# Linear-attention layers: two value tiles moved behind the last segment's keys, the first queries' features begun sooner, feature transposes in the two-bank logits tile

## The chip, the cores and the metric

The kernel runs on one core of a Trainium2 chip, as one launch with nothing computed on the host. A core has engines that run at the same time, each with its own instruction stream: PE (TensorE, matrix products and transposes), DVE (VectorE), ACT (ScalarE), POOL (GpSimd) and SP (SyncE, which here issues the transfers). They wait for each other on semaphores. PE writes its products to PSUM, from which DVE and ACT read them; everything else lives in SBUF, and what does not fit goes out to DRAM and comes back. The metric is the device time of one execution in microseconds (us), the median over runs.

## What is computed

A tensor x of 2048 rows (tokens) by 512 columns passes four layers: a linear-attention layer A, a segmented memory-attention layer B, then A and B again with the same weights, each on the layer-normed x and added back to it. There are 32 heads of 16 columns. The change lies in layer A alone:

```python
qkv = x @ wqkv                                   # 512 -> 3 * 512, split into q, k, v of 32 heads x 16
pq  = einsum("bhsd,hdf->bhsf", q, w_phi)         # a 16x16 matrix per head
pk  = einsum("bhsd,hdf->bhsf", k, w_phi)
phi_q = concat([softmax(pq), softmax(-pq)])      # 32 features per head
phi_k = concat([softmax(pk), softmax(-pk)])
kv  = einsum("bhsf,bhsd->bhfd", phi_k, v)        # summed over all 2048 tokens
z   = einsum("bhsf->bhf", phi_k)
num = einsum("bhqf,bhfd->bhqd", phi_q, kv)
den = einsum("bhqf,bhf->bhq", phi_q, z)[..., None] + 1e-6
out = (num / den) @ wo                           # heads side by side again
```

Nothing of `num` can be computed before `kv` holds all tokens, so layer A has two passes.

## The kernel before

**Layer A, first pass** (`LayerA.pass1`). The rows are worked in four segments of four tiles of 128 rows; the segments go in the order 1, 2, 3, 0. For a tile t of a segment, `kproj` and `qproj` multiply the transposed normalised rows by the key or query weights (with the per-head matrix folded in) into a PSUM tile "g", and ACT copies it to SBUF: keys to "U", queries to "tb". `v_tile` makes the value rows of a whole segment, four tiles with 12 matmuls each, in 16 steps (four a tile: three times four matmuls, then ACT's copy). The values of the coming segment are interleaved with the keys and queries of the present one by a list, `plan`: its entries say behind which step of the projections a step of the values, of the norms or of the transposes is taken. Of a query or key tile the features are made in four stages: `extremes` (DVE: maximum and minimum of each head, to `mmq` or `mm`), `differences` (two POOL instructions, to a fresh tile of the pool "P"), `exp` (ACT, in place, 128x1024), and the scaling by the reciprocal sums, `scale_q` for queries (DVE sums `es` and reciprocals `rr`, then one POOL multiplication) and `scale_k` for keys. `kv(0)` and `kv(1)` multiply key features with values into the PSUM tiles mx and my, and DVE adds them to `kva`.

The queries of the first three segments are stored in DRAM unfeatured (`pq`) and come back in the second pass. Those of the last segment, which holds the rows 0 to 511 and so the first four tiles of the second pass, stay in SBUF (`later`), and `begun(t)` takes their extremes and differences: for tiles 0 to 2 in full, for tile 3 the extremes alone.

**Layer A, second pass** (`LayerA.pass2`). At its front `kva` is transposed by PE ("g<-ident,kva") and masked by DVE into `KN`. Then, for each of 16 tiles: `transposed` turns the 128x1024 query features by eight 128x128 PE transposes, in two halves of four, each half copied by ACT to SBUF ("P<-g"); the product with `KN` (32 small matmuls, "g<-KN,P") in two halves; `weigh` divides by the denominator (DVE: reciprocal `r`, product `tmp`); `turn` transposes `tmp` (four PE transposes, "g<-ident,tmp"), which ACT rounds to `oh` and DVE completes by the rest `ol`; `out_proj` multiplies by the output weights (12 matmuls, "g<-w,oh" and "g<-w,ol"), and DVE adds x and SP stores the row tile. The loop runs one tile ahead: in an iteration i PE does turn(i-1), KN(i), transposes(i+1), out_proj(i-1), except for i = 1 and 2, where the transposes stand behind out_proj.

In the second pass's latter half the opening work of the following layer B (norms, projections, first logits) is mixed in at listed steps, and 103 of the second pass's steps run before layer B proper begins; the few that are left are taken in B's first slots.

**What sets the order.** Each engine runs its instructions in the order in which the program writes them: the wrapper `Ordered` (all its instructions carry line L163) and `held` (PE's: L185 for `mm`, L189 for `tp`) tie each instruction behind the one before it on its engine. Waits between engines follow from reads and writes of the same tiles.

**PSUM.** "g" is a set of three tiles of one bank (2 KB a partition) that rotate; "lg" is one tile of two banks, which layer B uses for its logits; mx, my and pv have a bank each:

```python
pt = PS("g", G)                    # one bank, one of three
lg = PS("lg", 1, (P, 2, 512))      # two banks, a single tile
```

**SBUF.** The pool "P" has six buffers of 128x1024, for features and for their transposes; "tb" (raw queries) and "U" (raw keys) two each.

Of the kernel before, what the change touches and what calls it, by code (L numbers as in the profile page):

```python
# [18 lines left out]
P = 128  # L19
NSEG = 4  # L20
# [87 lines left out]
def interleave_kernel(ctx, tc, x_in, a_wqkv, a_wphi, a_wo, b_wq, b_wk, b_wv, b_wo, b_beta,  # L108
# [78 lines left out]
    def tp(*a):  # L187
        work[0] += 108
        return held(nc.tensor.transpose(*a))  # L189
# [371 lines left out]
    def exp(e):  # L561
        ef = e.rearrange("p h s f -> p (h s f)")
        act.activation(ef, ef, AF.Exp)
# [24 lines left out]
    class LayerA:  # L588
# [68 lines left out]
        def pass1(self, first):  # L657
# [35 lines left out]
            for n, s in enumerate(SEGS):  # L693
# [51 lines left out]
                if n < NSEG - 1:  # L745
# [2 lines left out]
                    plan = [(j, g) for j in ((0, 2, 3, 4, 4, 8, 9, 11, 13) if n == 0 and not first else (4, 7, 10, 13))]  # L748
                    vals, norms = [10 + j * 26 // 16 for j in range(16)], (14, 19, 20, 21, 22, 23, 24, 27, 29, 31, 33)
                    vt = v_tile(hTs, wv, vv, ("g", G))  # L750
                    plan += [(j, vt) for j in vals]
                    if n + 2 < NSEG:
                        upc = upcoming(n + 2)
                        plan += [(j, upc[1]) for j in norms]
# [30 lines left out]
                        yield  # L785
                    for _, step in plan:
                        next(step, None)
                    late = kv(1)
                    continue

# [9 lines left out]

                for t in range(8):
                    yield from (kproj(t, e) if t < 4 else qproj(t - 4, e, later))
                    if t == 2:
                        yield from late
                        self.wo = load_w("awo")
                    if 0 < t < 5:
                        exp(e[t - 1])
                    if t in (5, 6):
                        add = kv(t - 5)
                        next(add)  # L810
                    if 1 < t < 6:
                        es.append(scale_k(e[t - 2]))
                    if t == 5:
                        yield from add
                        begun(0)
                    if t == 6:
                        begun(1)
                        exp(e[4])
                        yield from add
                        scale_q(e[4])  # L820

                pt = PS("g", G)
                for i in range(4):
# [2 lines left out]
                for j in (0, 2):  # L826
# [1 line left out]
                                      in0=pt.rearrange("p (g x) -> p g x", x=PW)[:, :, 0 : 2 * VW].rearrange(  # L828
                                          "p g (h e) -> p g h e", e=VW),
                                      in1=bdA[:, j : j + 2].unsqueeze(1).unsqueeze(3).broadcast_to([P, 8, 2, VW]))  # L830
                exp(e[5])
                scale_q(e[5])
                begun(2)
                begun(3)
                self.e = {4 * s + t: e[4 + t] for t in range(3)}
                yield

# [6 lines left out]
        def pass2(self):  # L844

            KN = self.KN
            phT = {}

            def transposed(i):

                if i >= NT:
                    return
                ef = self.e.pop(i).rearrange("p h s f -> p (h s f)")
                phT[i] = T2("P4", NP4, shape=(P, 8, P))
                for half in range(2):
                    pt = PS("g", G)
                    for q in range(4):
                        g = 4 * half + q  # L860
                        tp(pt[:, q * P : (q + 1) * P], ef[:, g * P : (g + 1) * P], ident)
                    act.copy(phT[i][:, 4 * half : 4 * half + 4, :], pt.rearrange("p (g t) -> p g t", g=4))
                    yield

            yield from transposed(0)
            o = None
            for i in range(NT + 1):
                if i > 0:
                    oT = turn([o[:, c * P : (c + 1) * P] for c in range(NC)])
                    yield PAUSE if i == NT else None  # L870
                if i + 2 < NT:
                    exp(self.e[i + 2])
                if i < NT:
                    o = T2("tmp", 2)
                    f = phT.pop(i)
                    for half in range(2):
                        pn = PS("g", G)
                        pv = pn[:, 0 : 16 * VW].rearrange("p (g h e) -> p g h e", g=4, h=4)
                        for q in range(4):
                            g = 4 * half + q  # L880
                            for a in (0, 64):
                                mm(pn[a : a + 64, q * 4 * VW : (q + 1) * 4 * VW], lhsT=f[:, g, a : a + 64],
                                   rhs=KN[:, g].rearrange("p h e -> p (h e)"), start=True, stop=True,
                                   tile_position=(0, a))
                        weigh(o[:, half * 256 : half * 256 + 256].rearrange("p (g h d) -> p g h d", g=4, h=4),
                              pv, 0.0, False)
                        yield
                    if not 0 < i < 3:
                        yield from transposed(i + 1)
                    if i + 2 < NT:  # L890
                        scale_q(self.e[i + 2])
                    if i + 3 < NT:
                        self.e[i + 3] = differences(*self.raw.pop(i + 3))
                    self.load_q(i + 4)
                    ahead = residual(self.xsrc, i, ("ot", OT))
                if i > 0:
                    yield from out_proj(x, self.xdst, i - 1, oT, self.wo)
                if 0 < i < 3:
                    yield from transposed(i + 1)
                x = ahead  # L900


# [468 lines left out]
```

## Time and profile before

| what | us |
|---|---|
| median of three runs | 1523.32 (1521.91 to 1523.49) |
| the profiled execution's own time | 1523.71 |
| its span in the trace | 1521.9 |
| PE busy | 1456.3 (96% of the span) |
| DVE busy | 1095.3 (72%) |
| ACT busy | 787.1 (52%) |
| POOL busy | 650.3 (43%) |

The 1.8 us between the span and the profiled execution's own time lie around the program. A row of a timeline gives the start in us, the duration in us, the engine, the line, the operation, what it writes and reads, the shapes and a count of instructions run together; in brackets stands the idle time of the engine just before, and what ended it. PEclk is the share of full clock that TensorE was granted. The profiled execution is one of several, and its parts carry its own delays.

In the first layer A the last segment's projections end at about 185.5 us and the second pass runs from there to about 313 us; the second layer A repeats this 743.8 us later.

### The profile page before, as it was taken

What the parts mean: (1) busy time and instruction counts of PE and PEld (TensorE: products, weight loads), DVE (VectorE), ACT (ScalarE), POOL (GpSimd) and SP (SyncE); (2) the same over time, 40 slices, a digit from 0 to 9 for tenths busy, and PEclk for the clock granted to TensorE, in tenths of its full rate; (3) what the DMA queues carried; (4) which work ended last, traced back from release to release, by engine and by line L of the source; (5) the groups of instructions that cost most, each with busy time, mean ns of one, the idle gap of its engine ahead of it and who ended that gap; (6) DMA issues with size and microseconds to landing.
All of it is one profiled execution on the core that took longest, in us unless ns stands there. A gap on an engine that the chain in (4) does not pass through costs nothing.

```text
span 1521.9 us, 30316 instructions
## 1 busy us (share of the span) xinstructions
PE 1456.3 (96%) x10888; PEld 1033.4 (68%) x10888; DVE 1095.3 (72%) x3258; ACT 787.1 (52%) x1178; POOL 650.3 (43%) x1000
## 2 busy tenths in 40 slices
PE   7999989999999999999999998999999999999998
PEld 6877767765666666666667786776656666666554
DVE  4765868668778877878656667757688788787783
ACT  5554335436565566556544333443565656655553
POOL 1668654313454544433314445541344445444331
PEclk9999999999999999999999999999999999999999
DMA  5487265545444443535340122744463353443340
GB/s 183 129 289 254 70 210 165 167 119 153 122 110 117 135 104 103 157 99 147 114 143 33 39 84 80 225 148 144 113 175 106 105 153 99 111 118 98 80 112 36
DMA packets 108773, 195.85 MB, mean 129 GB/s; under 512 B 14416, under 2 KB 27856, under 8 KB 107856
## 3 DMA queue, kind: packets, MB, share of 16 engines
q1 hardware_dynamic: 107472, 193.38, 42.8%
q8 instruction: 88, 1.44, 0.4%
q10 hardware_dynamic: 1152, 0.52, 0.1%
q14 instruction: 61, 0.50, 0.1%
HBM read 101.05 MB, written 39.85 MB: 93 GB/s over the span
## 4 chain that ended last, share of the span: by engine, by line
PE 78%; DVE 12%; ACT 4%; issue 2%; POOL 2%; DMA 1%; SPq 0%; ACTq 0%; POOLq 0%; DVEq 0%
PE g L185 45%; PE pv L185 9%; PE lg L185 9%; PE g L189 7%; PE mx L185 5%; PE my L185 3%; DVE mx L163 2%; POOL P L163 2%; DVE es L163 2%; ACT P L163 1%; DVE my L163 1%; DVE mxs L163 1%; ACT tb L163 1%; DVE hl L163 1%; DVE ol L163 1%
## 5 line engine op out<-in xcount | busy, mean ns | idle before, releaser
L163 ACT ACTIVATE P<-lg 128x1024 f32<-128x1024 f32 x320 | 328.9, 1028 | 173.0 <-PE lg L185 165.5
L163 POOL TENSOR_SCALAR_AFFINE_SELECT P<-P 128x256 f32<-128x256 f32 (+1 forms) x448 | 190.7, 440 | 442.3 <-ACT P L163 441.7
L163 DVE CUSTOM_DVE_ANT_0 mx<-mx,mask 128x128 f32<-128x128 f32 (+3 forms) x512 | 255.3, 499 | 160.7 <-PE my L185 109.0
L163 DVE CUSTOM_DVE_ANT_0 my<-my,mask 128x128 f32<-128x128 f32 (+3 forms) x512 | 265.9, 519 | 6.5
L185 PE MATMUL g<-hh,wqk 128*128 128x512 f32 x512 | 180.5, 407 | 2.1 <-ACT hh L163 1.4
L185 PE MATMUL lg<-e,e 64*128 64x256 f32 (+2 forms) x1024 | 168.4, 387 | 7.8 <-ACT P L163 7.6
L185 PE MATMUL g<-w,oh 128*128 128x512 f32 x512 | 170.6, 414 | 3.5 <-DVE ol L163 1.6
L185 PE MATMUL pv<-P,v 128*32 128x512 f32 (+3 forms) x2048 | 165.0, 441 | 0.0
L185 PE MATMUL my<-e,e 63*128 63x256 f32 (+2 forms) x512 | 146.7, 346 | 5.3 <-DVE mxs L163 3.9
L185 PEld LDWEIGHTS lg<-e,e 64*128 64x128 f32 x1024 | 81.1, 184 | 103.2 <-issue 50.6
L185 PE MATMUL g<-w,hh 128*128 128x512 f32 x448 | 145.8, 406 | 0.9 <-ACT tb L163 0.9
L163 DVE DVE_READ_ACCUMULATOR2_ANT mxs<- 128x1 f32 x1024 | 145.0, 142 | 0.0
L185 PE MATMUL mx<-e,e 63*128 63x256 f32 (+2 forms) x512 | 140.8, 330 | 0.2
L185 PEld LDWEIGHTS pv<-P,v 128*32 128x32 f32 x2048 | 53.7, 109 | 100.9 <-issue 92.0
L185 PEld LDWEIGHTS g<-hh,wqk 128*128 128x128 f32 x512 | 96.3, 188 | 24.0 <-ACT hh L163 1.8
L185 PEld LDWEIGHTS g<-w,oh 128*128 128x128 f32 x512 | 89.4, 190 | 30.9 <-issue 5.7
L185 PE MATMUL g<-w,ol 128*128 128x512 f32 x256 | 101.8, 398 | 0.0
L185 PE MATMUL g<-hl,wqk 128*128 128x512 f32 x256 | 100.4, 392 | 0.4 <-DVE hl L163 0.4
L163 POOL TENSOR_SCALAR tb<-tb 128x512 f32<-128x512 f32 x48 | 71.5, 1489 | 67.4 <-ACT tb L163 67.4
L163 ACT CAST ta<-g 128x512 fp32r<-128x512 f32 x64 | 37.6, 587 | 112.5 <-PE g L185 112.2
L185 PEld LDWEIGHTS my<-e,e 63*128 63x128 f32 x512 | 82.0, 185 | 18.1 <-DVE mxs L163 8.8
L185 PEld LDWEIGHTS mx<-e,e 63*128 63x128 f32 x512 | 89.7, 186 | 6.1 <-issue 3.6
(143 smaller groups left out, 2816.8 us busy)
## 6 DMA issues: line engine op xcount, KB each, us to landing
e<-ta SPq DMA_DIRECT2D x384, 128.0 KB
wqk<-wqk SPq DMA_DIRECT2D x64, 512.0 KB
x<-x SPq DMA_DIRECT2D x48, 256.0 KB
ot<-in SPq DMA_DIRECT2D x28, 256.0 KB
pq<-tb SPq DMA_DIRECT2D x24, 256.0 KB
tb<-pq SPq DMA_DIRECT2D x24, 256.0 KB
x<-xr SPq DMA_DIRECT2D x24, 256.0 KB
xr<-x SPq DMA_DIRECT2D x24, 256.0 KB
```

What stands on the lines that cost most here:

```text
L163: i = f(*a, **k)
L185: return held(nc.tensor.matmul(*a, **k))
L189: return held(nc.tensor.transpose(*a))
```

## The change

It has three parts, all in layer A.

1. **Values.** In segment 2's plan only the first 8 of the 16 steps of the last segment's values are taken (two of its four tiles). The other two tiles are made in the last segment, one behind the projection of key tile 3, one behind that of query tile 0.
2. **First queries' features.** In the last segment, `begun(0)` and `begun(1)` come behind the projection of query tile 1 and ahead of the first addition to `kva`; then follow both exponentials and the scaling of tile 0. `begun(2)` comes behind the projection of query tile 2, and the scaling of tile 1 behind the second addition. `begun(3)` (with its two DVE reductions) moves into the second pass, behind the division of tile 0. In the loop the differences of tile i+3 come ahead of the scaling of tile i+2, which for i = 1 stands behind the transposes of tile 2.
3. **Banks.** `transposed` puts its two halves into the two banks of one "lg" tile in place of two "g" tiles.

```diff
@@ LayerA.pass1, the plan of segments 0 to 2
                     vt = v_tile(hTs, wv, vv, ("g", G))
-                    plan += [(j, vt) for j in vals]
+
+                    plan += [(j, vt) for j in vals[: 16 if n + 2 < NSEG else 8]]
...
                     for _, step in plan:
                         next(step, None)
+                    rest = vt if n + 2 == NSEG else None
                     late = kv(1)
                     continue
...
                 for t in range(8):
                     yield from (kproj(t, e) if t < 4 else qproj(t - 4, e, later))
+                    if t in (3, 4):
+                        for _ in range(4):
+                            next(rest)
+                            yield
                     if t == 2:
                         yield from late
                         self.wo = load_w("awo")
...
                     if t == 5:
+                        begun(0)
+                        begun(1)
                         yield from add
-                        begun(0)
+                        exp(e[4])
+                        exp(e[5])
+                        scale_q(e[4])
                     if t == 6:
-                        begun(1)
-                        exp(e[4])
+                        begun(2)
                         yield from add
-                        scale_q(e[4])
+                        scale_q(e[5])
...
-                exp(e[5])
-                scale_q(e[5])
-                begun(2)
-                begun(3)
+                self.begun = begun
                 self.e = {4 * s + t: e[4 + t] for t in range(3)}
                 yield
@@ LayerA.pass2
                 phT[i] = T2("P4", NP4, shape=(P, 8, P))
+                pt = PS("lg", 1, (P, 2, 512))
                 for half in range(2):
-                    pt = PS("g", G)
                     for q in range(4):
                         g = 4 * half + q
-                        tp(pt[:, q * P : (q + 1) * P], ef[:, g * P : (g + 1) * P], ident)
-                    act.copy(phT[i][:, 4 * half : 4 * half + 4, :], pt.rearrange("p (g t) -> p g t", g=4))
+                        tp(pt[:, half, q * P : (q + 1) * P], ef[:, g * P : (g + 1) * P], ident)
+                    act.copy(phT[i][:, 4 * half : 4 * half + 4, :], pt[:, half].rearrange("p (g t) -> p g t", g=4))
                     yield
...
                     if not 0 < i < 3:
                         yield from transposed(i + 1)
-                    if i + 2 < NT:
-                        scale_q(self.e[i + 2])
+                    if i == 0:
+                        self.begun(3)
                     if i + 3 < NT:
                         self.e[i + 3] = differences(*self.raw.pop(i + 3))
+                    if i != 1 and i + 2 < NT:
+                        scale_q(self.e[i + 2])
...
                 if 0 < i < 3:
                     yield from transposed(i + 1)
+                if i == 1:
+                    scale_q(self.e[i + 2])
```

DVE's stream between the first layer A's two passes, before the change (mmq is what `extremes` writes; es, rr belong to a query tile's scaling; P_314 holds the features of tile 0, P_318 those of tile 1):

```order
L163 TENSOR_TENSOR kva_434<-mx_1902,kva_434 128x512
L163 TENSOR_REDUCE mmq_432<-tb_308_1879 128x32 x2
L163 TENSOR_REDUCE mmq_432<-tb_311_1900 128x32 x2
L163 TENSOR_TENSOR kva_434<-my_1961,kva_434 128x512
L163 TENSOR_REDUCE es_2001<-P_314_1943 128x64
L163 RECIPROCAL rr_2003<-es_2001 128x32
L163 TENSOR_TENSOR rr_2003<-rr_2003,es_2001 128x32
L163 TENSOR_TENSOR KN_2027<-g_2022,bd 128x8x34 x2
L163 TENSOR_REDUCE es_2031<-P_318_1996 128x64
L163 RECIPROCAL rr_2033<-es_2031 128x32
L163 TENSOR_TENSOR rr_2033<-rr_2033,es_2031 128x32
L163 TENSOR_REDUCE mmq_432<-tb_316_1959 128x32 x2
```

The same place after it, with the features of tile 0 in P_314 and those of tile 1 in P_315:

```order
L163 TENSOR_REDUCE mmq_432<-tb_307_1865 128x32 x2
L163 TENSOR_REDUCE mmq_432<-tb_311_1900 128x32 x2
L163 TENSOR_TENSOR kva_434<-mx_1902,kva_434 128x512
L163 TENSOR_REDUCE es_1953<-P_314_1942 128x64
L163 RECIPROCAL rr_1955<-es_1953 128x32
L163 TENSOR_TENSOR rr_1955<-rr_1955,es_1953 128x32
L163 TENSOR_REDUCE mmq_432<-tb_319_1972 128x32 x2
L163 TENSOR_TENSOR kva_434<-my_1974,kva_434 128x512
L163 TENSOR_REDUCE es_2013<-P_315_1947 128x64
L163 RECIPROCAL rr_2015<-es_2013 128x32
L163 TENSOR_TENSOR rr_2015<-rr_2015,es_2013 128x32
L163 TENSOR_TENSOR KN_2039<-g_2034,bd 128x8x34 x2
```

The first two tiles' extremes stand ahead of the first addition to `kva`, the sums of both tiles ahead of `KN`, those of tile 2 (tb_319) ahead of the second addition, and those of tile 3 are no longer in the stretch.

PE's stream in an iteration of the second pass that repeats (turn, product with KN, transposes of the next tile, output projection), before the change; in brackets stand the engines whose semaphores an instruction waits on:

```order
L189 MATMUL g_2429<-ident,tmp_2361 128x128 [waits Activation_49]
L189 MATMUL g_2429<-ident,tmp_2361 128x128 x3
L185 MATMUL g_2438<-KN_2027,P_407_2386 64x68 [waits Activation_49]
L185 MATMUL g_2438<-KN_2027,P_407_2386 64x68 x7
L185 MATMUL g_2450<-KN_2027,P_407_2386 64x68 [waits DVE_49]
L185 MATMUL g_2450<-KN_2027,P_407_2386 64x68 x7
L189 MATMUL g_2472<-ident,P_395_2327 128x128 [waits DVE_49,Pool_49]
L189 MATMUL g_2472<-ident,P_395_2327 128x128 x3
L189 MATMUL g_2478<-ident,P_395_2327 128x128 [waits DVE_49,PE_49]
L189 MATMUL g_2478<-ident,P_395_2327 128x128 x3
L185 MATMUL g_2497<-w_1823,oh_2427 128x512 [waits DVE_49,PE_49,Activation_49]
```

The product with KN, the transposes and the start of the output projection of such an iteration after the change:

```order
L185 MATMUL g_2432<-KN_2039,P_402_2381 64x68 [waits PE_49]
L185 MATMUL g_2432<-KN_2039,P_402_2381 64x68 x7
L185 MATMUL g_2444<-KN_2039,P_402_2381 64x68 [waits DVE_49,Activation_49]
L185 MATMUL g_2444<-KN_2039,P_402_2381 64x68 x7
L189 MATMUL lg_2466<-ident,P_388_2316 128x128 [waits PE_49,Pool_49]
L189 MATMUL lg_2466<-ident,P_388_2316 128x128 x3
L189 MATMUL lg_2466<-ident,P_388_2316 128x128 [waits Activation_49]
L189 MATMUL lg_2466<-ident,P_388_2316 128x128 x3
L185 MATMUL g_2490<-w_1795,oh_2421 128x512 [waits DVE_49]
```

Before, the two halves of the transposes are written to two tiles (g_2472 and g_2478), and neither waits for ACT; after, both are written to one (lg_2466), and the second half waits on ACT's semaphore, at the count that ACT's copy of the first half of the same tile, lg_2466, raises.

## Prediction

> **What bounds the kernel now.** I read the page first, for the engine shares and the chain that ended last, then busy time by stretches for the stages that the change touches, then the rows of PE and of its releasers there.
>
> ```profile
> PE 1456.3 (96%) x10888; PEld 1033.4 (68%) x10888; DVE 1095.3 (72%) x3258; ACT 787.1 (52%) x1178; POOL 650.3 (43%) x1000
> PE 78%; DVE 12%; ACT 4%; issue 2%; POOL 2%; DMA 1%; SPq 0%; ACTq 0%; POOLq 0%; DVEq 0%
> 166.00:186.00 20.00, 20.00 (x238) 16.59 (x233) 17.62 (x24) 6.57 (x9) 14.76 (x13) 1.00 0.12 42
> 186.00:205.00 19.00, 12.07 (x142) 9.63 (x140) 13.52 (x30) 7.60 (x13) 10.32 (x10) 0.94 0.41 132
> 205.00:268.00 63.00, 58.41 (x541) 45.36 (x537) 46.78 (x100) 31.27 (x49) 30.75 (x35) 0.99 0.61 187
> 930.00:949.00 19.00, 13.30 (x141) 10.74 (x140) 13.50 (x30) 7.58 (x13) 10.34 (x10) 0.85 0.41 133
> ```
>
> PE is busy 96% of the span and carries 78% of the chain: what the change is worth is PE time, added, saved or waited. (A stretch's row gives length, PE busy time and count, then weight loads, DVE, ACT, POOL, granted clock, DMA share, GB/s.) In the last segment (166 to 186) PE has no idle time. At the second pass's front it works 12.07 of 19.00 us in the first layer A and 13.30 in the second, so 6.9 and 5.7 us are idle there: all that sooner features could save. From 205 to 268, seven iterations that repeat and three with other work between, PE works 58.41 of 63.00.
>
> **Part 1, the values.** It removes and adds no PE instruction: 24 matmuls go from behind segment 2's last projections to behind the last segment's third key and first query tile. Both places lie where PE is always busy (20.00 of 20.00 above), so the move costs PE nothing and the projections end where they did, at 185.5. Cover gone, its price would be a gap at the new place, and I see none: values are needed by the products with keys, behind them. It brings the last key tile forward: I put that tile's sums at 174.8 where they were at 177.14 (below), one value tile sooner. The output weights' load stands on SP, whose queue also carries the second pass's x and query loads, and waits for the weight buffer that is now read later; in the second layer A to about 173. Two tiles of 1.05 MB at the 187 GB/s that the row 205 to 268 moved are 11 us, so it lands near 184, before the first output projection (196.16). Zero, and a rival's share if not.
>
> **Part 2, the front.** These rows stand for the first layer A before; DVE, ACT and POOL first, then PE:
>
> ```profile
> 177.14 1.21 DVE L163 TENSOR_REDUCE es<-P 128x64 f32<-128x1024 f32 x1
> 180.18 2.46 DVE L163 TENSOR_REDUCE mmq<-tb 128x32 f32<-128x512 f32 x4
> 184.76 1.22 DVE L163 TENSOR_REDUCE es<-P 128x64 f32<-128x1024 f32 x1 [1.27 <-ACT P L163]
> 186.51 0.78 DVE L163 TENSOR_TENSOR KN<-g,bd 128x272 f32<-128x272 f32 x2
> 183.59 1.06 ACT L163 ACTIVATE P<-P 128x1024 f32<-128x1024 f32 x1
> 181.00 1.06 POOL L163 TENSOR_TENSOR P<-tb,mmq 128x512 f32<-128x512 f32 x1 [0.39 <-DVE mmq L163]
> 185.54 0.60 PE L189 MATMUL g<-ident,kva 128*128 128x128 f32 x4
> 187.87 1.09 PE L189 MATMUL g<-ident,P 128*128 128x128 f32 x8 [1.73 <-POOL P L163]
> 189.20 1.18 PE L185 MATMUL g<-KN,P 128*64 128x68 f32 x32 [0.24 <-ACT P L163]
> 196.16 0.73 PE L185 MATMUL g<-w,oh 128*128 128x512 f32 x2 [0.81 <-DVE ol L163]
> 202.36 0.89 PE L189 MATMUL g<-ident,tmp 128*128 128x128 f32 x4 [2.27 <-DVE xr L163]
> 203.18 2.08 PE L185 MATMUL g<-KN,P 128*64 128x68 f32 x32
> 208.46 1.04 PE L189 MATMUL g<-ident,P 128*128 128x128 f32 x8
> 209.41 0.66 PE L189 MATMUL g<-ident,tmp 128*128 128x128 f32 x4
> 219.04 0.70 PE L185 MATMUL g<-w,oh 128*128 128x512 f32 x2
> 221.91 0.60 PE L189 MATMUL g<-ident,tmp 128*128 128x128 f32 x4
> 946.33 0.76 PE L189 MATMUL g<-ident,tmp 128*128 128x128 f32 x4 [2.27 <-DVE xr L163]
> ```
>
> In the new order DVE takes the extremes of tiles 0 and 1 (2.46 us for both, row 180.18) at once behind the key work, 177.2 to 179.7, with nothing of `kva` ahead. POOL's differences of tile 0 start at 178.6 (before 181.00), two instructions of 1.06 a tile; ACT's exponentials stand at 180.7 and 182.75 (tile 0's before at 183.59); tile 0's sums are through before the last query tiles arrive. What is late next is `kva`: its second addition now stands behind the extremes of tile 2, whose copy on ACT stands behind both exponentials (183.7). Extremes 184.4 to 185.7, addition to 186.3; so `kva` is transposed at 186.4 where it was at 185.54, a new wait of 0.9 on PE. Then the sums of tile 1 stand ahead of the two multiplications for KN (1.75 from the start of 184.76 to that of 186.51, then 0.78), and KN is there at 188.85: the first product starts 0.35 sooner than 189.20, though tile 0's features had been ready long before.
>
> From there I follow PE with the durations of these rows (product 1.18; turn 0.5, the 0.60 of row 221.91 less its overlap with the product behind; output projection 2.87, from 219.04 to 221.91; transposes of a tile 1.90 by part 3): tile 1's transposes 190.1, turn 192.0, product 192.5, output projection 194.7 (it still waits for DVE's rest; before 196.16), tile 2's transposes 197.6, second turn 199.5. That turn stood at 202.36 behind an idle 2.27 for DVE's addition of x, which held the one-bank tile that the turn needs; with the transposes out of the set of three, the turn takes the bank of a product, long free. Then product 200.0, output projection 201.75 (it waits for DVE's rest, as before), tile 3's transposes 204.6 and the third turn at 206.5 where it was 209.41: 2.9 us sooner. The second layer A has the same wait (row 946.33, 2.27), and I take 2.9 there too. Bounds: from 1.5 us later (the 0.9 of `kva` and 0.6 more, were each of the next waits to stay) to the 6.9 and 5.7 idle in all.
>
> The clock bears on this.
>
> ```profile
> 202.00:204.00 2.00, 1.64 (x18) 1.31 (x20) 0.40 (x2) 0.59 (x1) 2.00 (x3) 0.66 0.89 314
> ```
>
> Right behind the stretch without products (199.5 to 203) the granted clock is 0.66 in this row, and the product there takes 2.08 (row 203.18) instead of 1.18. I leave about 0.9 a layer of the gain resting on it. [...]
>
> **Part 3, the banks.** Where a tile's transposes ended before:
>
> ```profile
> 209.16 1.07 ACT L163 COPY P<-g 128x512 f32<-128x512 f32 x2 [3.13 <-PE g L189]
> 216.23 1.17 PE L185 MATMUL g<-KN,P 128*64 128x68 f32 x32
> 217.70 1.06 ACT L163 ACTIVATE P<-P 128x1024 f32<-128x1024 f32 x1 [0.78 <-POOL P L163]
> 217.79 1.25 PE L189 MATMUL g<-ident,P 128*128 128x128 f32 x8 [0.39 <-POOL P L163]
> 218.67 1.05 ACT L163 COPY P<-g 128x512 f32<-128x512 f32 x2
> 256.11 1.25 PE L189 MATMUL g<-ident,P 128*128 128x128 f32 x8
> 257.35 0.70 PE L185 MATMUL g<-w,oh 128*128 128x512 f32 x2
> 291.40 1.13 PE L189 MATMUL g<-ident,P 128*128 128x128 f32 x8
> 292.73 0.73 PE L185 MATMUL g<-w,oh 128*128 128x512 f32 x2 [0.20 <-ACT P L163]
> 311.47 1.09 PE L189 MATMUL g<-ident,P 128*128 128x128 f32 x8
> 312.80 0.50 PE L185 MATMUL g<-w,oh 128*128 128x512 f32 x1 [0.24 <-ACT P L163]
> ```
>
> PE is ready for tile 5's transposes at 217.40 (216.23 plus 1.17), waits 0.39 for POOL and a bank, and the output projection starts at 219.04: 1.64 us from ready to next. So with tiles 4 to 10. Tile 11 takes 1.24 (256.11 to 257.35), and tile 12 as long; tiles 13 and 15 take 1.33 (291.40 to 292.73, 311.47 to 312.80).
>
> After the change the order's row of the second half waits for ACT's copy of the first, since both are one tile. A wait of this kind stands once in before, where the second half had no bank:
>
> ```profile
> 298.85 0.65 PE L189 MATMUL g<-ident,P 128*128 128x128 f32 x4
> 299.61 0.57 ACT L163 COPY P<-g 128x512 f32<-128x512 f32 x1
> 300.23 0.66 PE L189 MATMUL g<-ident,P 128*128 128x128 f32 x4 [0.73 <-ACT P L163]
> 300.82 0.50 PE L185 MATMUL mx<-e,e 63*128 63x512 f32 x1
> ```
>
> The first half starts at 298.85, the copy runs 299.61 to 300.18, the second half starts at 300.23 and the next work at 300.82. With ACT free the copy starts 0.70 behind the transposes (208.46 to 209.16), so a tile costs 0.70 + 0.57 + 0.05 + 0.59 = 1.91; I use 1.90. Lower bound: no wait, 0.95 for eight transposes in a row (208.46 to 209.41). Upper bound: 2.48, the exponential still ahead of the copy (below). I take 1.90, the row of the same wait, since the differences now stand ahead of the scaling on POOL, and so the exponential comes earlier and leaves ACT free when the first half ends.
>
> Against before: seven tiles (4 to 10) by 0.26, two by 0.66, two by 0.57, tile 14 (1.97 before) by -0.07: 1.82 + 1.32 + 1.14 - 0.07 = 4.2 us a layer. Tiles 0 to 3 are in part 2. Some of it falls into waits that stand anyway, the longest behind tile 14:
>
> ```profile
> 306.88 0.69 PE L185 MATMUL g<-KN,P 128*64 128x68 f32 x16 [0.83 <-DVE xr L163]
> ```
>
> DVE's addition, late by layer B's work, holds this product 0.83; I let half be absorbed, 0.4 a layer. The price of 1.90 has no cover in the repeating iteration: the next PE work, the output projection, stands behind it in order.
>
> [...] The row 298.85 to 300.82 speaks for the wait.
>
> **Sum.** Parts: 0 for the values, -2.9 x 2 for the front, +4.2 x 2 for the banks, -0.4 x 2 absorbed: +1.8 us. Against the profiled execution's own 1523.71 that is 1525.5; against the median of 1523.32, +2.2 us or 0.14%. From no change a measurement of this kernel can tell about 0.2%, 3.05 us: below 1520.3 is faster, above 1526.4 slower.
>
> **Rivals.**
> - *The front gives less (slower).* Part of the 2.9 is the clock's 0.9 and the rest hangs on DVE's order; if `kva` comes later than 186.4 (its DVE queue holds the extremes of tile 2 and, behind it, tile 1's sums), KN and all behind it shift one for one. With 1.7 a layer: 1525.5 + 2.4 = 1527.9. It is slower from 2.5 a layer down. For it: DVE is busy 13.52 of 19.00 in the front; against: the 2.27 wait goes whatever `kva` does.
> - *The halves overlap (faster).* If the second half does not wait, a tile costs 0.95: tiles 4 to 10 gain 0.69 each, 11 and 12 0.29, 13 and 15 0.38, 14 1.0, in sum 7.2 a layer, and the front 2 more than above: -2 x (7.2 + 4.9) = -24, 1499.5. Against it: the order's wait, and the row 300.23.
> - *The exponential stays in front of the copy (slower).* Its place is ACT in each iteration: at 217.70 it took 1.06, and the copies followed at 218.67. If it still starts there, the first copy ends at 219.24, the second half at 219.88, and a tile costs 2.48: seven tiles by 0.58 more, 4.1 a layer, 1533.7. It decides once the exponential starts less than 0.36 before the first half's copy is due, more than 0.35 later than I assume. Against: its differences need a feature buffer freed one iteration before and no longer the scaling.
> - *The front gives more (faster).* If KN comes at 187 and no clock drop is left, the front could give 6 a layer: 1523.71 - 12 + 7.6 = 1519.3. Against: DVE's sums of tile 1 stand ahead of KN.
> - *Nothing:* the front's waits move but end where they did, and the half's wait is absorbed, so 1523.7. For it, little; it lies within the forecast's bounds.
>
> **Chances.** My forecast with its bounds (front 2.5 to 4.5, price 1.8 to 2.0) 0.42, the front less 0.27, the exponential 0.10, the front more 0.12, the halves overlapping 0.03, nothing 0.06. The forecast gives mostly no change that can be told (0.34) and some slower (0.08); of "less" 0.05 is still the same, of "more" 0.02. Faster is then 0.10 + 0.03 = 0.13, the same 0.34 + 0.05 + 0.02 + 0.06 = 0.47, slower 0.08 + 0.22 + 0.10 = 0.40. For the range, low is the front giving 6 a layer, 1519.3; high is the front at 1.7 and a third of the exponential's price, 1527.9 + 2.6 = 1530.5. By itself the forecast runs from 1522 to 1527.
>
> **What would show it.** Each second half of "lg<-ident,P" starts about 1.3 us behind its first, with an idle of about 0.7 for ACT; from one product with KN to the next the repeating iteration takes 0.26 longer; the 2.27 waits at 202.36 and 946.33 are gone; `kva` is transposed near 186.4 and the third turn starts near 206.5. The forecast is wrong if the halves follow each other at 0.5 us, if copies start over 0.9 behind their transposes, or if KN is not there by 189.

## The result and the profile after

The changed kernel takes 1520.95 us in the median of 14 runs (1518.71 to 1523.34), the kernel before beside it 1522.49 (14 runs): a ratio of 0.9986 with a 95% interval of 0.9978 to 0.9993. That is 0.14% faster: small, but the interval stays below 1. The prediction had 0.14% slower.

The page of the changed kernel, engine shares and the chain that ended last:

```profile
PE 1448.3 (95%) x10888; PEld 1030.5 (68%) x10888; DVE 1095.1 (72%) x3258; ACT 788.3 (52%) x1178; POOL 649.9 (43%) x1000
PE 81%; DVE 9%; ACT 5%; issue 2%; DMA 1%; POOL 1%; SPq 0%; ACTq 0%; POOLq 0%; DVEq 0%
```

PE is still what bounds the kernel; its part of the chain has grown from 78% to 81%, and DVE's has fallen from 12% to 9%. The stretches of the front and of the iterations behind it (columns as in the prediction):

```profile
186.00:205.00 19.00, 15.44 (x163) 11.97 (x161) 15.16 (x33) 8.05 (x12) 11.20 (x12) 1.00 0.62 191
205.00:268.00 63.00, 54.00 (x527) 43.55 (x527) 43.58 (x94) 30.68 (x48) 30.31 (x36) 1.00 0.56 169
930.00:949.00 19.00, 15.40 (x162) 11.93 (x160) 15.15 (x33) 8.17 (x13) 11.20 (x12) 1.00 0.60 204
```

In the front PE now works 15.4 of 19 us in both layers, where it worked 12.07 and 13.30, at the full clock where it had 0.94 and 0.85. From 205 to 268 it works 54.00 of 63 where it worked 58.41: the waits have moved from the front into the iterations. Rows of the timeline that match in both traces show how the lead goes (the lead is how much earlier the changed kernel reaches the same instruction). Of the kernel before, a reduction ahead of the change's place, a transpose of layer B's opening behind tile 12's, and the third turn in the second layer A:

```profile
136.20 1.28 DVE L163 TENSOR_REDUCE mmq<-tb 128x32 f32<-128x512 f32 x2 [2.01 <-ACT tb L163]
266.06 0.60 PE L189 MATMUL g<-ident,x 128*128 128x128 f32 x4
953.39 0.66 PE L189 MATMUL g<-ident,tmp 128*128 128x128 f32 x4
```

Of the changed kernel the same three, PE's steps of the first front and the start of the second between them:

```profile
136.88 1.28 DVE L163 TENSOR_REDUCE mmq<-tb 128x32 f32<-128x512 f32 x2 [2.33 <-ACT tb L163]
186.68 0.63 PE L189 MATMUL g<-ident,kva 128*128 128x128 f32 x4 [0.20 <-DVE kva L163]
189.02 1.42 PE L185 MATMUL g<-KN,P 128*64 128x68 f32 x32
199.50 0.60 PE L189 MATMUL g<-ident,tmp 128*128 128x128 f32 x4
206.26 0.60 PE L189 MATMUL g<-ident,tmp 128*128 128x128 f32 x4
264.46 0.60 PE L189 MATMUL g<-ident,x 128*128 128x128 f32 x4
930.41 0.63 PE L189 MATMUL g<-ident,kva 128*128 128x128 f32 x4
950.01 0.60 PE L189 MATMUL g<-ident,tmp 128*128 128x128 f32 x4
```

Ahead of the change the profiled execution of the changed kernel runs 0.68 us late (136.88 against 136.20). At the third turn it is 3.15 us early (206.26 against the prediction's row 209.41): the front gained 3.8. Behind tile 12 it is 1.60 early (264.46 against 266.06): tiles 4 to 12 gave 1.55 back. In the second layer the third turn is 3.38 early (950.01 against 953.39), and by matching rows the execution had come to that layer's front 0.75 late: 4.1 gained.

One repeating iteration of the changed kernel, PE's rows and ACT's copy:

```profile
218.77 0.60 PE L189 MATMUL g<-ident,tmp 128*128 128x128 f32 x4
219.30 1.21 PE L185 MATMUL g<-KN,P 128*64 128x68 f32 x32
220.44 0.66 PE L189 MATMUL lg<-ident,P 128*128 128x128 f32 x4
221.13 0.58 ACT L163 COPY P<-lg 128x512 f32<-128x512 f32 x1 [0.18 <-PE lg L189]
221.77 0.66 PE L189 MATMUL lg<-ident,P 128*128 128x128 f32 x4 [0.68 <-ACT P L163]
222.18 0.71 PE L185 MATMUL g<-w,oh 128*128 128x512 f32 x2
225.05 0.60 PE L189 MATMUL g<-ident,tmp 128*128 128x128 f32 x4
```

The second half waits 0.68 for ACT's copy of the first, as forecast. In most tiles it is this wait (0.73 in some of the front); at tile 10 it is 1.09 in both layers, since ACT still works on a row of layer B's opening (246.32, 0.80 us) when the half is ready. From turn to turn the iteration takes 6.28 us, where it took 6.21 (215.70 to 221.91 before): 0.07 more, not 0.26.

The rest of the lead goes at about 307 us and again at 1051. Stretches of 3.41 us of the changed kernel, the one ahead of 307.01 and the two at these places:

```profile
303.60:307.01 3.41, 1.95 (x36) 1.50 (x35) 3.31 (x12) 0.85 (x2) 0.65 (x1) 1.00 0.21 84
307.01:310.43 3.42, 3.42 (x9) 2.66 (x9) 0.27 (x1) 0.00 (x0) 0.00 (x0) 0.50 0.01 3
1051.12:1054.53 3.41, 3.41 (x9) 2.68 (x9) 0.26 (x1) 0.00 (x0) 0.00 (x0) 0.50 0.03 8
```

At 307.01 and 1051.12 the granted clock halves for one stretch, under matmuls that keep PE busy all the time. By rows that match in both traces, the lead of the first layer falls there from 1.39 us to 0.22 behind. The kernel before has such stretches elsewhere, one in the first layer's front, two in the second's and one near the end of the program:

```profile
202.64:206.05 3.41, 3.41 (x38) 2.85 (x37) 1.96 (x5) 1.64 (x2) 2.29 (x3) 0.50 0.79 258
933.09:936.50 3.41, 3.08 (x37) 2.58 (x38) 3.34 (x9) 0.34 (x1) 3.08 (x3) 0.50 0.00 0
946.74:950.16 3.42, 3.42 (x38) 2.83 (x37) 2.09 (x6) 1.64 (x2) 2.17 (x3) 0.50 0.80 233
1492.88:1496.29 3.41, 3.41 (x21) 1.25 (x20) 0.56 (x1) 1.41 (x3) 0.56 (x2) 0.50 0.03 5
```

### The profile page after: what moved, and what is told of

Same layout as the page of the kernel before. It is cut to its first block, busy times and chain, and to the rows that moved or that the text cites. A ratio compares the mean times of both kernels' runs of the same rounds, so it can differ in the third digit from the quotient of the medians.

```text
span 1521.3 us, 30293 instructions
## 1 busy us (share of the span) xinstructions
PE 1448.3 (95%) x10888; PEld 1030.5 (68%) x10888; DVE 1095.1 (72%) x3258; ACT 788.3 (52%) x1178; POOL 649.9 (43%) x1000
## 4 chain that ended last, share of the span: by engine, by line
PE 81%; DVE 9%; ACT 5%; issue 2%; DMA 1%; POOL 1%; SPq 0%; ACTq 0%; POOLq 0%; DVEq 0%
PE g L185 47%; PE pv L185 9%; PE lg L185 8%; PE g L189 6%; PE mx L185 5%; PE my L185 3%; PE lg L189 2%; DVE mx L163 2%; ACT P L163 2%; DVE my L163 1%; DVE es L163 1%; DVE mxs L163 1%; DVE hl L163 1%; DVE mmq L163 1%; ACT tb L163 1%
```

## The experiments

Each was timed beside the kernel before on the same chip; ratios are to that, with the 95% interval.

**Parts 1 and 2 without part 3.** The transposes stay in the "g" tiles:

```diff
 (the changed kernel, transposed)
-                pt = PS("lg", 1, (P, 2, 512))
                 for half in range(2):
+                    pt = PS("g", G)
...
```

> The changed kernel with its transposes back in the one-bank g tiles (parts 1 and 2 alone). Theory 1: the front's gain comes from DVE's new order, in which the addition of x stands ahead of the sums of tile 3, so the second turn finds its bank free; the gain of 3.2 us a layer stays, the repeating iterations run at 6.21 us as before, and the kernel is about 6 us under before. Theory 2: the gain comes from the transposes leaving the set of three banks; then the second turn again waits some 2 us for the addition of x, and the kernel is 1 to 3 us under before.

Measured 1514.41 us, ratio 0.9947 (0.9934 to 0.9961): 8 us faster. PE's rows of the first turns:

```profile
199.18 0.66 PE L189 MATMUL g<-ident,tmp 128*128 128x128 f32 x4
205.35 0.66 PE L189 MATMUL g<-ident,tmp 128*128 128x128 f32 x4
```

The second turn (199.18) follows the transposes with no wait, though they and it still share the "g" banks: the addition of x now stands ahead of the sums of tile 3. Theory 1 holds: DVE's new order is enough to take the 2.27 us wait away. Against the changed kernel (0.9986) part 3 costs 0.39% on top of parts 1 and 2, some 6 us. Part of that lies in the front: this execution is 1.24 us late at the reduction of 136.20 (137.44) and 4.06 early at the third turn (205.35 against 209.41), so without the banks the front gains 5.3 us, where the changed kernel gains 3.8.

**Part 3 alone.** The kernel before with the changed kernel's `transposed`:

```diff
+                pt = PS("lg", 1, (P, 2, 512))
                 for half in range(2):
-                    pt = PS("g", G)
...
```

> Part 3 alone, on the kernel before. Theory of the prediction: a tile costs 1.90 us, 4.2 us a layer from tile 4 on, so about 6 to 8 us slower than before, less what the front's turn gains. Theory from the trace after: a tile costs 1.8 us from where PE is ready, the repeating iteration 6.27 us against 6.21, some 1.5 to 2 us a layer, and the turn's 2.27 us wait goes (its bank is no longer that of the output projection): within 2 us of before.

Measured 1534.52 us, ratio 1.0077 (1.0064 to 1.0090): 12 us slower, more than either theory. Up to some 4 us of it may be the clock's, by an estimate: the median granted clock of these runs is 0.9945 where the kernel before has 0.997, and 0.0025 of 1530 us is 3.8 us if PE were busy throughout. The second turn, and the second half of the transposes in two iterations:

```profile
203.16 0.60 PE L189 MATMUL g<-ident,tmp 128*128 128x128 f32 x4
219.76 0.66 PE L189 MATMUL lg<-ident,P 128*128 128x128 f32 x4 [0.78 <-ACT P L163]
240.34 0.66 PE L189 MATMUL lg<-ident,P 128*128 128x128 f32 x4 [1.90 <-ACT P L163]
```

The second turn (203.16) has no wait here either, so the banks alone would have taken it away too. But the halves' waits are 0.78 and 1.90 in these rows, and 2.35 at tile 1 (194.78), where the changed kernel mostly has 0.68: the copy of the first half is late on ACT. In the changed kernel something in part 2 makes it early.

**What makes it early.** The changed kernel with POOL's old order in the loop:

```diff
-                    if i + 3 < NT:
-                        self.e[i + 3] = differences(*self.raw.pop(i + 3))
                     if i != 1 and i + 2 < NT:
                         scale_q(self.e[i + 2])
+                    if i + 3 < NT:
+                        self.e[i + 3] = differences(*self.raw.pop(i + 3))
```

> The changed kernel with POOL's scaling of tile i+2 ahead of the differences of tile i+3, as before. Theory 1: the differences ahead of the scaling are what frees ACT for the first half's copy; undone, the exponential stands in front of the copy, the second half waits 0.8 to 1.9 us instead of 0.68, and the kernel is 3 to 6 us slower than the changed one. Theory 2: the exponential is early enough either way, and the time is the changed kernel's within 1.5 us.

Measured 1524.13 us, ratio 1.0006 (0.9997 to 1.0016), where the changed kernel has 0.9986 in one session and 0.9985 in the other.

```profile
214.47 1.06 ACT L163 ACTIVATE P<-P 128x1024 f32<-128x1024 f32 x1 [0.69 <-POOL P L163]
215.43 0.57 ACT L163 COPY P<-lg 128x512 f32<-128x512 f32 x1
216.05 0.66 PE L189 MATMUL lg<-ident,P 128*128 128x128 f32 x4 [1.18 <-ACT P L163]
236.21 0.66 PE L189 MATMUL lg<-ident,P 128*128 128x128 f32 x4 [1.49 <-ACT P L163]
```

The second halves wait 1.18 and 1.49. Theory 1 holds: the exponential, released by POOL only at 214.47, stands ahead of the copy (215.43) for which PE waits. The swap alone is worth 3.2 us (0.21%) to the changed kernel.

**The second half without its wait.** All eight transposes ahead of the two copies, in the same "lg" tile:

```diff
-                for half in range(2):
-                    for q in range(4):
-                        g = 4 * half + q
-                        tp(pt[:, half, q * P : (q + 1) * P], ef[:, g * P : (g + 1) * P], ident)
+                for g in range(8):
+                    tp(pt[:, g // 4, g % 4 * P : (g % 4 + 1) * P], ef[:, g * P : (g + 1) * P], ident)
+                for half in range(2):
                     act.copy(phT[i][:, 4 * half : 4 * half + 4, :], pt[:, half].rearrange("p (g t) -> p g t", g=4))
```

> The changed kernel with all eight transposes of a tile issued ahead of the two copies, so that the second half no longer waits for the first half's copy. Theory 1: that wait is PE time that nothing covers, a tile goes from 1.8 to about 0.95 us, the repeating iteration from 6.27 to 5.4 us, and the kernel ends near 1500 us. Theory 2: the next wait stands right behind (DVE's rest for the output projection, or POOL's features), the iteration stays above 6 us and the kernel within 5 us of the changed one.

Measured 1504.44 us, ratio 0.9878 (0.9864 to 0.9893).

```profile
212.06 0.60 PE L189 MATMUL g<-ident,tmp 128*128 128x128 f32 x4
217.45 0.60 PE L189 MATMUL g<-ident,tmp 128*128 128x128 f32 x4
230.34 0.69 PE L185 MATMUL g<-KN,P 128*64 128x68 f32 x16 [0.90 <-DVE ot L163]
```

The iteration falls to 5.39 us (212.06 to 217.45): theory 1. The wait was there because the code wrote the second bank of a tile after its first had been read; that PE can write one bank while ACT copies another, the kernel before shows with two tiles (217.79 to 219.04 the transposes, 218.67 the first copy, in the prediction's rows). In the changed kernel too the halves lie in two banks, and its trace shows no overlap (221.13 to 221.71 the copy, 221.77 the next half). Here the copies run under the output projection (they start at 220.24, it at 219.96), not under the other half. Behind it a new wait appears, 0.90 at 230.34, for DVE's addition of x, which holds a "g" bank.

**The eight transposes without parts 1 and 2.** The same edit on the kernel before, whose `pt` becomes the "lg" tile ahead of the loop:

> The kernel before with all eight transposes of a tile in the two-bank tile and ahead of the two copies, without parts 1 and 2. Theory 1: the parts add up; it is 8 to 11 us faster than before. Theory 2: without the earlier exponential the copies come late for the next product with KN, which then waits for ACT, and no more than 3 us are gained.

Measured 1518.49 us, ratio 0.9965 (0.9951 to 0.9979): 5 us, between the two theories.

```profile
213.36 1.22 DVE L163 TENSOR_REDUCE es<-P 128x64 f32<-128x1024 f32 x1 [1.65 <-ACT P L163]
215.11 0.69 DVE L163 TENSOR_TENSOR ot<-g,ot 128x512 f32<-128x512 f32 x1
215.95 0.69 PE L185 MATMUL g<-KN,P 128*64 128x68 f32 x16 [0.63 <-DVE ot L163]
235.39 0.69 PE L185 MATMUL g<-KN,P 128*64 128x68 f32 x16 [1.47 <-DVE ot L163]
```

The product's second half waits (0.63 at 215.95, 1.47 at 235.39), not for ACT as theory 2 said, but for a bank that DVE's addition of x holds. That addition (215.11) stands behind the sums of a coming tile (213.36), which wait 1.65 for the late exponential. Eight transposes and the new order together gain 19 us, apart 5 and 8.

**Part 1 alone.** On the kernel before:

```diff
-                    plan += [(j, vt) for j in vals]
+                    plan += [(j, vt) for j in vals[: 16 if n + 2 < NSEG else 8]]
...
+                    if t in (3, 4):
+                        for _ in range(4):
+                            next(rest)
+                            yield
```

> Part 1 alone, on the kernel before: two value tiles behind the last segment's key 3 and query 0. Theory 1: PE is busy throughout, nothing else waits on it, so the time is before's within 1 us. Theory 2: the last key tile's features, 2.4 us sooner, bring the addition to kva and the first queries' features forward on DVE, 1 to 2 us a layer.

Measured 1523.78 us, ratio 1.0001 (0.9992 to 1.0010): theory 1, nothing by itself.

**Part 2 alone.** Parts 1 and 2 with the values put back:

```diff
-                    plan += [(j, vt) for j in vals[: 16 if n + 2 < NSEG else 8]]
+                    plan += [(j, vt) for j in vals]
...
-                    if t in (3, 4):
-                        for _ in range(4):
-                            next(rest)
-                            yield
```

> Part 2 alone: the features' new order, with the transposes in the g tiles and the values where they were. Theory 1: part 1, worth nothing alone, is needed here: without it the last key's sums come 2.4 us later and push the first queries' extremes, exponentials and with them kva; some 2 us a layer of the 8.8 that parts 1 and 2 gain together are lost. Theory 2: DVE has room enough, and the time is that of parts 1 and 2 within 1.5 us.

Measured 1519.19 us, ratio 0.9972 (0.9962 to 0.9982); with part 1 it is 0.9947. `kva` comes late:

```profile
180.76 2.46 DVE L163 TENSOR_REDUCE mmq<-tb 128x32 f32<-128x512 f32 x4
189.48 0.63 PE L189 MATMUL g<-ident,kva 128*128 128x128 f32 x4 [2.60 <-DVE kva L163]
```

The extremes of the first two tiles start at 180.76, where they start at 178.52 with part 1 (the run with parts 1 and 2), and PE waits 2.60 us for `kva`, where it waits 0.20 there. Theory 1 holds: part 1, free and useless alone, is worth some 4 us to part 2.

**The clock again.** The changed kernel, unaltered, in a second profile:

> The changed kernel once more, for a second profile. Theory 1: the two stretches of half clock in its first profile (307 and 1051 us, some 1.6 us each) hang on where the windows of the clock happen to fall; here they are absent or elsewhere, and without them the second pass ends some 1.5 us a layer ahead of before's. Theory 2: they belong to the changed kernel and stand at the same places again, and the gain of the front is spent there in every execution.

Measured 1520.58 us, ratio 0.9985 (0.9976 to 0.9993). The stretches that answer to 307.01 and 1051.12 in the first profile, and the one ahead of the second:

```profile
306.99:310.40 3.41, 3.41 (x10) 2.64 (x9) 0.19 (x1) 0.00 (x0) 0.00 (x0) 0.50 0.01 2
1047.69:1051.10 3.41, 1.94 (x29) 1.48 (x24) 2.98 (x9) 0.45 (x2) 0.06 (x1) 1.00 0.21 79
1051.10:1054.51 3.41, 3.12 (x16) 2.02 (x14) 0.84 (x3) 0.84 (x2) 0.00 (x0) 1.00 0.21 24
```

The half clock is there again at 306.99, but not at 1051. Ahead of the first place the program runs 0.1 us earlier than in the first profile, ahead of the second 0.6, while the grid on which such stretches lie (below) is the same to 0.02 us. So each theory has one of the two places; that the same code takes the half clock in one execution and not in the other speaks for theory 1, that it hangs on where the windows, stretches of 3.41 us in the traces, fall. How often they fall so, an estimate from the other runs' clocks tells roughly: one stretch at half clock lowers a run's mean granted clock by 0.0011 (half of 3.41 in 1520 us), and the changed kernel's 25 runs list clocks from 0.997 to 1.000, so none to some three stretches in a run.

**Further along.** The kernel with eight transposes, its first eleven output projections written to the bank pv:

```diff
-    def out_proj(x, xdst, i, o, w):
-        po = PS("g", G)
+    def out_proj(x, xdst, i, o, w, tag=("g", G)):
+        po = PS(*tag)
...
-                    yield from out_proj(x, self.xdst, i - 1, oT, self.wo)
+                    yield from out_proj(x, self.xdst, i - 1, oT, self.wo, ("pv", PV) if i < 12 else ("g", G))
```

> The kernel with eight transposes ahead of the copies, with the first eleven output projections written to the bank pv in place of a g tile. Theory 1: the waits of a product's second half for DVE's addition of x (0.90 and 0.62 us near 230 and 236) are waits for the bank; they go, 1.5 to 2 us a layer. Theory 2: DVE's own order sets the pace there, the wait returns in front of the output projection, and the time stays within 1 us.

Measured 1501.43 us, ratio 0.9845 (0.9827 to 0.9863). The iteration is 5.35 us (221.95 to 227.30), and the 0.90 wait is gone, as theory 1 has it: it was for the bank. The next is 0.42 for POOL:

```profile
221.95 0.60 PE L189 MATMUL g<-ident,tmp 128*128 128x128 f32 x4
227.30 0.60 PE L189 MATMUL g<-ident,tmp 128*128 128x128 f32 x4
234.75 1.09 PE L189 MATMUL lg<-ident,P 128*128 128x128 f32 x8 [0.42 <-POOL P L163]
```

Last, the same kernel with DVE's second addition to `kva` and the products for KN moved ahead:

```diff
                     if t == 6:
-                        begun(2)
                         yield from add
-                        scale_q(e[5])
+                        begun(2)
...
                                       in1=bdA[:, j : j + 2].unsqueeze(1).unsqueeze(3).broadcast_to([P, 8, 2, VW]))
+                scale_q(e[5])
                 self.begun = begun
```

> The kernel with eight transposes ahead of the copies and the output projections in pv, and in the front DVE's second addition to kva ahead of the extremes of tile 2 and the products for KN ahead of the sums of tile 1. Theory 1: kva and the sums ahead of KN hold the first product (0.94 us of wait there, and kva itself 0.9 late); it comes 1 to 2 us sooner, and the kernel gains 2 to 4 us. Theory 2: tile 1's features, then later, are the next to be waited for, and the time stays within 1 us.

Measured 1498.78 us, ratio 0.9840 (0.9826 to 0.9853), not to be told from 0.9845 by these intervals.

```profile
188.02 1.19 PE L185 MATMUL g<-KN,P 128*64 128x68 f32 x32 [0.68 <-ACT P L163]
190.30 1.62 PE L189 MATMUL lg<-ident,P 128*128 128x128 f32 x8 [1.09 <-POOL P L163]
```

The first product waits 0.68 for ACT instead of 0.94 for DVE, and 1.09 us of waiting for POOL's features of tile 1 stands right behind it (eight transposes take 1.62 us there, where those at 186.31 take 1.04, and the turn behind them, at 191.71, takes 1.06, where the one at 198.22 takes 0.60; that this is a stretch of half clock is an estimate from these rows): theory 2, mostly. It is the fastest of these kernels in its median, and both it and the one ahead of it beat the kernel before and the changed kernel.

## Why the prediction was right or wrong

*Part 1, zero.* Right as to its place and price (ratio 1.0001 alone). That it brings the last key's sums forward was used in part 2's schedule, and there it decides: without it 4 us are lost.

*Part 2, the front, -2.9 a layer.* The schedule held: `kva` transposed at 186.68 (forecast 186.4), first product at 189.02 (188.85), second turn at 199.50 (199.5), third turn at 206.26 (206.5), the 2.27 wait gone. The gain was undersized all the same: 3.8 us in the first layer and about 4.1 in the second. The forecast compared its 206.5 with 209.41 as though both executions had come to the front at the same time; the changed one came 0.68 later. Counted from there, `kva` was transposed 0.46 late (186.68 less 0.68, against 185.54) where 0.9 was forecast, and the way from it to the third turn took 19.58 us where the forecast had 20.1. The second layer differs from the first in `kva` alone, which is only 0.16 late there (930.41 less 0.75, against 929.50): from it to the third turn PE needs 23.87 and 23.89 us in the two layers before the change, 19.58 and 19.60 after it. The stretch of half clock at 933.09, which only the second front has before the change, cost nothing on that way. The reason given for the 2.27, that the transposes leave the set of banks, is half of it: the wait goes with the banks alone, and goes as well with the transposes kept in the set, since the addition of x moved ahead on DVE.

*Part 3, the banks, +4.2 a layer.* This is the step that failed, by its size. The mechanism is as forecast: each second half waits for ACT, mostly 0.68 us. But the repeating iteration, forecast 0.26 longer, is 0.07 longer, and a tile costs 1.74 from the start of its transposes to the output projection (220.44 to 222.18), not 1.90: the last four transposes take 0.41 until the next matmul starts, where 0.59 was taken from a row with a product of another kind behind it (300.23 to 300.82), and the first start 0.07 before the product's modelled end (219.30 plus 1.21 against 220.44). Tiles 4 to 12 cost 1.55 us instead of 3.1: 0.17 for tiles 4 to 9 together (the lead falls from 3.15 to 2.98 at the turn of tile 8, 244.25 against 247.23), and 0.49, 0.44 and 0.45 for tiles 10, 11 and 12, the first by its wait of 1.09, the others because such a tile took 1.24 before where tiles 4 to 10 took 1.64 (the prediction's rows), with no wait in it that the new one could replace. From tile 13 on the price was about 0.6 a layer with what DVE absorbs, near the 0.7 of the forecast. Together 2.2 a layer against 3.8. That is not all that the banks cost: their waits at tiles 0 to 3 lie in the front's term, where the run without them gains 1.5 us more. That run gives back 0.45 behind the third turn (a lead of 4.06 falls to 3.61 at the turn of tile 14, 312.77 against 316.38), so a layer pays about 1.5 + 2.2 - 0.45 = 3.2 for the banks, which is the 6 us of the two runs' times.

*The sum.* With the measured terms: -3.8 and -4.1 for the fronts, +2.2 twice for the banks, -3.5 us against a profiled execution of 1523.71, so 1520.2 where the median is 1520.95. The changed kernel's own profiled execution took 1523.0, with two stretches of half clock at the second passes' ends, some 1.6 us each, that the sum had nowhere; in the second profile, with one of them, it took 1520.56. The terms were off by 5.3 us together, all to the side of too slow; that this execution came within 2.5 us of the forecast 1525.5 is in good part the luck of those two stretches.

*The rivals.* The front gave more, as the rival with 0.12 said, but 3.8 to 4.1 and not 6. The exponential in front of the copy was a rival for the changed kernel with 0.10; it did not happen, and the swap on POOL is why: with it undone the second halves wait 1.18 and 1.49 and 3.2 us are lost. Part 3 alone costs 12; how much of that is the exponential's no run separates. The halves that overlap (1499.5, 0.03) did not happen; with all eight transposes ahead of the copies no half waits, a tile costs 0.85 (219.11 to 219.96 in that run) and the time is 1504.44.

*The clock.* In the new front PE does nothing but transposes from 186.68 to 189.02, and neither profile shows a drop there or behind it: in the first the granted clock of 186 to 205 is 1.00, in the second the product at 192.62 takes 1.17 us, where 2.08 was measured at half the clock (the prediction's row 203.18). The drops came at the end of the second pass (307.01 and 1051.12), where nothing was forecast. In the run of part 2 alone the 3.41 us from 188.19 have no other PE work than transposes (189.48 to 190.98) and a clock of 1.00, and the product behind them (191.91) takes 1.17 us too:

```profile
188.19:191.60 3.41, 1.50 (x12) 1.29 (x12) 3.34 (x7) 1.02 (x3) 2.46 (x3) 1.00 0.03 9
```

The clock also bears on the sign of the result. Beside the second profile the median granted clock is 0.997 in the runs of the kernel before (21) and 0.999 in those of the changed kernel (11). The difference of 0.002 is worth up to 3.0 us (an estimate: 0.002 of 1520 us, were PE busy throughout), and the medians differ by 3.2 (1523.75 and 1520.58). Whether the changed kernel would be faster at an equal clock stays open: no run here holds the clock fixed.

## What to carry to other kernels

Here a two-bank tile rotated nothing while its second bank was written after its first had been read (0.68 us of wait in most tiles): with all the writes issued, then the reads, the wait was gone, 16 us for the move of two lines. A buffer edit and a reordering are not worth the sum of their parts: the same part 3 cost 12 us on the old order and 6 on the new, and of that difference the swap on POOL, which takes an exponential out from in front of a copy, was measured at 3.2; the values' move was worth 0 or 4. When an edit is priced at a few tenths of a us a tile, take each term from a row with the same instruction behind it, and look at where the next instruction starts, not at when this one ends.

## What the hardware showed that was not expected

A stretch of half clock lasts 3.41 us in these traces, and in the profiles that show several all lie on one grid: in the kernel before they start at 202.64, 933.09, 946.74 and 1492.88, of which the last three are 730.45, 744.10 and 1290.24 us behind the first, that is 214, 218 and 378 times 3.4133; in the first profile of the changed kernel 307.01 and 1051.12 are 744.11 apart, 218 times 3.4133. The grid's place differs between executions (the first stretch's remainder is 1.25 before, 3.22 and 3.20 in the changed kernel's two), and the same kernel in its second profile has one such stretch less.

What sets one off, PE's busy time in the stretch ahead does not tell. Ahead of the drop at 307.01 PE is busy 1.95 of the 3.41 us (row 303.60 above), with the 64-column matmuls of a product, some transposes, and a wait of 1.18 us:

```profile
305.58 0.69 PE L185 MATMUL g<-KN,P 128*64 128x68 f32 x16 [1.18 <-DVE xr L163]
307.52 1.05 PE L185 MATMUL g<-hh,wqk 128*128 128x512 f32 x2
```

Half the clock follows (two matmuls in 1.05 us, where two with the same tiles take 0.62 at 266.79, at the full one). Ahead of the first drop before, from 199.23, PE was busy 1.14 of 3.41. Ahead of the stretch at 1492.88 in the kernel before PE was busy 2.23 of 3.41 us, and half the clock followed; with 1.50 in part 2 alone (above) and with 1.94 at 1047.69 in the changed kernel's second profile the full clock stayed:

```profile
1489.47:1492.88 3.41, 2.23 (x15) 1.24 (x13) 0.68 (x2) 2.49 (x4) 2.21 (x5) 1.00 0.00 0
```

What does decide it, no run here tells.
